# VectorE's instructions as one loop over the heads in a one-query attention kernel

## The chip, the cores and the metric

One core of one Trainium2 chip. The metric is the time of one execution on the device in microseconds (us), the median of several executions. "Span" is the part of it that the profile covers, from the first to the last instruction; it is about 2 us shorter.

## The reference

```python
B, Hq, Hkv, Sq, Sk, D = 1, 32, 8, 1, 65536, 128       # q, k, v in bf16
k = jnp.repeat(k, 4, axis=1); v = jnp.repeat(v, 4, axis=1)
scores = jnp.einsum("bhqd,bhkd->bhqk", q, k) * D ** -0.5
p = softmax(scores, axis=-1)
return jnp.einsum("bhqk,bhkd->bhqd", p, v)
```

One query row per head, 8 groups of 4 query heads, and 65536 keys and values each. K and V together are 268.4 MB, and every byte is used once.

## The kernel before

A head is one of the 8 groups. Its K comes in two tiles of 8.4 MB, and so does its V. VectorE transposes K in place, PE computes scores, VectorE and PE find the maximum, ScalarE takes the exps, VectorE transposes these ("weights"), and PE multiplies them with V. There are three tile buffers in `io`: one for V, two for K. SyncE issues each load when its buffer is free again.

```python
def load_v(g, b):
    done = 2 * (2 * g + b)
    ...                                         # last tiles in pieces
    else:
        SP.wait((s_vc, done))                   # values of the tile before are finished
        load(v, g, b, 0, s_v[0])
        sp.sem_inc(s_v[1], 16)
...
def collect(last=False):                        # "product" and "sum"
    n = DV.mark(dve.tensor_tensor(out=..., in0=vacc, in1=sely..., op=ALU.mult))
    DV.after(n)
    if not last:
        return DV.mark(dve.tensor_reduce(out=vs[:, 0:D], in_=vy[:, :, :], axis=AX.X, op=ALU.add))
...
for g in range(G):                              # unrolled: 8 heads
    for _ in transposes(g, 0): pass
    for i, _ in enumerate(transposes(g, 1)):
        if i == 0 and g:
            DV.wait((s_vc, 4 * g - 2)); weights(g - 1, 1)
    top(g)
    softmax(g)
    if 0 < g < G - 1:
        weights(g, 0)
        DV.wait((s_vc, 4 * g))
        collected[g - 1] = collect()
        ACTQ.wait((s_dv, collected[g - 1]))
        clear(g)                                # ScalarE writes zeros into acc
    elif g: ...
    else:
        weights(g, 0)                           # head 0: nothing to collect
```

PE runs a loop of its own over the tiles. After it comes the end of the last V tile. Its last 24 keys are multiplied one at a time ("singles", a weight load and a 128-column matmul each), and a last fp32 matmul (the "gather") adds what the wide matmuls summed:

```python
for t in range(SL - TAIL, SL):                  # TAIL = 24
    if t in CUTS: pe.wait_ge(s_v[CUTS.index(t)], 16)
    ...
    pe.matmul(out=fin, lhsT=et[:, 1, w0:w0 + H], rhs=io[:, t, :], ...)
pe.wait_ge(s_dv, collected[G - 1])
gather(D, start=False, stop=True).then_inc(s_pe, 1)
```

ScalarE then scales the 4x128 result ("scaling") and stores it.

## Time and profile before

| | before |
|---|---|
| time, median of 3 | 629.8 us (629.76 to 630.69) |
| span of the profiled run | 628.1 us |
| load queue, share of 16 engines | 99.1% |
| first load packet, last load packet | 1.99, 624.47 us |
| last load packet to scaling / scaling to the end of the store / end of the store to the end | 1.10 / 1.22 / 1.35 us |

The page of the kernel before: the span, busy time by engine, the tenths by slice for the DMA engines, and the queue of the loads.

```profile
span 628.1 us, 7091 instructions
PE 346.7 (55%) x2120; PEld 136.0 (22%) x2120; DVE 339.2 (54%) x132; ACT 36.1 (6%) x32; POOL 7.5 (1%) x40
...
DMA  8999999999999999999999999999999999999996
...
q1 hardware_dynamic: 6656, 268.45, 99.1%
```

No compute engine is busy over 55%, and the DMA engines are always busy. The same kernel by stretches (start:end, length, busy us and number of instructions by engine, granted PE clock, DMA share, GB/s):

```profile
core 0: us, PE busy (x) PEld busy (x) DVE busy (x) ACT busy (x) POOL busy (x), PEclk, DMA share, GB/s
2.00:624.00 622.00, 345.25 (x2102) 135.00 (x2102) 337.94 (x129) 35.14 (x31) 6.41 (x33) 0.82 1.00 431
618.00:622.00 4.00, 1.37 (x21) 0.35 (x16) 0.00 (x0) 0.00 (x0) 0.00 (x0) 1.00 0.98 393
622.00:626.00 4.00, 3.08 (x38) 1.68 (x38) 1.48 (x4) 0.36 (x1) 0.00 (x0) 1.00 0.42 142
```

The first row says that 622 of 628 us are loads at a DMA share of 1.00. So only three things can change the time: the rate of the stream, a hole in it, and its two ends.

A middle head (timeline: start, duration, engine, line, operation, and in brackets the idle time before and what ended it):

```profile
363.87 1.97 ACT L247 ACTIVATE ex<-acc,nmb 128x2048 bf16<-128x2048 f32 x1 [68.70 <-DVE nmb L245]
365.96 1.25 DVE L269 STREAM_TRANSPOSE et<-ex 128x1024 bf16<-128x1024 bf16 x1 [2.13 <-ACT ex L247]
367.13 1.01 DVE L275 TENSOR_TENSOR vy<-acc,sely 128x512 f32<-128x512 f32 x1
368.18 0.69 DVE L281 TENSOR_REDUCE vs<-vy 128x128 f32<-128x512 f32 x1
368.90 2.31 ACT L258 ACTIVATE acc<-wz 128x2560 f32<-128x2560 bf16 x1 [2.97 <-DVE vs L281]
371.68 0.59 PE L374 MATMUL pf<-vs,sel 128*4 128x130 f32 x2 [8.04 <-PEq L114]
```

After the exps come weights, product and sum on VectorE, then the clear on ScalarE, then PE's gather.

The end of the chain that ended last (start, duration, what):

```profile
623.56 0.61 PE pf L479 x8
624.17 0.03 issue
624.20 1.05 PE pf L479 x16
625.25 0.23 PE pf L374 x2
...
625.57 0.36 ACT o L341
```

Sixteen singles took 1.05 us, 66 ns each, then the gather.

### The profile page before, as it was taken

Reading aid. Unit: us, or ns where it says so; the run is one execution under the profiler, and the core shown is the slowest. Engines: PE = TensorE matmul, PEld = TensorE weight load, DVE = VectorE, ACT = ScalarE, POOL = GpSimd, SP = SyncE. Lnnn points to the kernel's source line nnn. Section 1 sums busy time; section 2 is a strip of 40 time slices with the busy share of each in tenths; the row PEclk is TensorE's granted clock in tenths of the full one; section 3 lists DMA queues with packets and bytes.
Section 4 is the critical chain, followed back from the end, with each engine's and each line's share of the span. In section 5 each row is a group of like instructions: output and inputs, shape, how many; then the busy total and the mean of one; then the engine's idle time right before and its main releaser. Section 6 shows DMA issues by size and latency. Waiting matters only on the chain. (4 is left out here: it accounts for less than half of the span.)

```text
span 628.1 us, 7091 instructions
## 1 busy us (share of the span) xinstructions
PE 346.7 (55%) x2120; PEld 136.0 (22%) x2120; DVE 339.2 (54%) x132; ACT 36.1 (6%) x32; POOL 7.5 (1%) x40
## 2 busy tenths in 40 slices
PE   0776473725838257382674816648076571876344
PEld 0322131311313023130221302213022230332112
DVE  3984836549065490654807558085570846684210
ACT  0000200020000200002000020000200002000100
POOL 1000000000000000000000000000000000000000
PEclk9999696976969769597695967969679696999658
DMA  8999999999999999999999999999999999999996
GB/s 368 434 467 401 467 401 467 401 447 422 426 442 430 438 430 438 430 438 426 442 413 455 409 459 401 467 401 467 401 463 405 463 405 463 402 435 434 434 434 271
DMA packets 6714, 268.48 MB, mean 427 GB/s; under 512 B 824, under 2 KB 1080, under 8 KB 1464
## 3 DMA queue, kind: packets, MB, share of 16 engines
q1 hardware_dynamic: 6656, 268.45, 99.1%
q8 instruction: 1, 0.02, 0.0%
q10 hardware_dynamic: 56, 0.01, 0.0%
q14 instruction: 1, 0.01, 0.0%
HBM read 268.44 MB, written 0.01 MB: 427 GB/s over the span
## 5 line engine op out<-in xcount | busy, mean ns | idle before, releaser
L422 PE MATMUL acc<-io,wz 128*128 x1024 | 268.5, 413 | 184.3 <-PEq L114 180.6
L228 DVE STREAM_TRANSPOSE io<-io 128x4096 uint32<-128x4096 uint32 (+1 forms) x54 | 279.1, 5207 | 164.7 <-DMA io<-in_k_dram 164.7
L422 PEld LDWEIGHTS acc<-io,wz 128*128 x1024 | 105.1, 103 | 347.8 <-issue 267.9
L380 PE MATMUL acc<-io,et 128*16 128x512 bf16 x1018 | 67.8, 409 | 23.6 <-PEq L114 22.2
L233 DVE TENSOR_REDUCE mg<-acc 128x1 f32<-128x2048 f32 x8 | 18.3, 2292 | 52.8 <-PE acc L422 52.8
L247 ACT ACTIVATE ex<-acc,nmb 128x2048 bf16<-128x2048 f32 x8 | 15.7, 1967 | 531.4 <-DVE nmb L245 531.4
L374 PE MATMUL pf<-vs,sel 128*4 128x130 f32 (+1 forms) x20 | 5.5, 374 | 62.6 <-PEq L114 62.6
L380 PEld LDWEIGHTS acc<-io,et 128*16 128x16 bf16 x1018 | 26.3, 94 | 62.1 <-issue 37.7
L269 DVE STREAM_TRANSPOSE et<-ex 128x1024 bf16<-128x1024 bf16 x16 | 19.6, 1225 | 29.5 <-ACT ex L247 14.9
L258 ACT ACTIVATE acc<-wz 128x2560 f32<-128x2560 bf16 x7 | 16.1, 2307 | 17.9 <-DVE vs L281 17.8
L374 PEld LDWEIGHTS pf<-vs,sel 128*4 128x4 f32 x20 | 1.2, 83 | 63.0 <-issue 63.0
L275 DVE TENSOR_TENSOR vy<-acc,sely 128x512 f32<-128x512 f32 x8 | 7.8, 980 | 12.0 <-PE acc L380 12.0
L237 DVE TENSOR_REDUCE m<-pt 1x4 f32<-1x128 f32 x8 | 2.2, 278 | 21.2 <-PE pt L464 21.2
L360 POOL COPY wz<-qT 32x16 bf16<-32x16 bf16 x32 | 6.1, 191 | 517.8 <-PE acc L422 435.3
L449 PE MATMUL pt<-et 128*16 128x512 bf16 x16 | 6.3, 395 | 0.0
L281 DVE TENSOR_REDUCE vs<-vy 128x128 f32<-128x512 f32 x7 | 4.8, 686 | 0.2
L466 PE MATMUL pb<-ident,nrow 1*128 1x1 f32 x8 | 1.5, 189 | 5.7 <-PEq L114 5.7
L464 PE MATMUL pt<-ident,mg 128*1 128x128 f32 x8 | 2.3, 283 | 2.5 <-PEq L114 2.5
L191 DVE MEMSET acc<- 128x2560 f32 x1 | 2.2, 2192 | 1.6 <-SPq L62 1.6
L245 DVE COPY nmb<-pb 128x1 f32<-128x1 f32 x8 | 1.3, 158 | 3.0 <-PE pb L466 3.0
L466 PEld LDWEIGHTS pb<-ident,nrow 1*128 1x128 f32 x8 | 1.1, 134 | 7.1 <-issue 7.1
L294 ACT ACTIVATE fall<-pf 4x130 f32<-4x130 f32 x7 | 1.9, 269 | 7.5 <-PE pf L374 7.5
(28 smaller groups left out, 16.4 us busy)
## 6 DMA issues: line engine op xcount, KB each, us to landing
io<-in_v_dram SPq DMA_DIRECT2D x5, 4096.0 KB, 16.8
io<-in_k_dram SPq DMA_DIRECT2D x4, 4096.0 KB, 25.9
io<-in_k_dram SPq DMA_DIRECT2D x4, 2048.0 KB, 40.3
io<-in_v_dram SPq DMA_DIRECT2D x1, 2048.0 KB, 10.7
io<-in_v_dram SPq DMA_DIRECT2D x1, 1024.0 KB, 12.9
io<-in_v_dram SPq DMA_DIRECT2D x3, 256.0 KB, 13.3
io<-in_v_dram SPq DMA_DIRECT2D x2, 128.0 KB, 13.2
io<-in_k_dram SPq DMA_DIRECT2D x13, 43.9
```

The source lines that it names most:

```text
L228: dve.transpose(out=part, in_=part).then_inc(s_kt, n // 32)
L233: dve.tensor_reduce(out=mg[:, :], in_=sc, axis=AX.X, op=ALU.max).then_inc(s_mg, 1)
L247: n = ACTQ.mark(act.activation(out=ex[:, :, :].rearrange("p b n -> p (b n)"), in_=sc, func=ACT.Exp, bias=nmb[:, :], scale=SCALE, accum_out ...
L258: cleared[g] = ACTQ.mark(act.activation(out=acc[:, :], in_=wz[:, 0, 0:1].to_broadcast([P, 5 * 512]), func=ACT.Copy))
L269: dve.transpose(out=et[:, :, :].rearrange("p i n -> p (i n)"), in_=ex[:, 2 * b:2 * b + 2, :].rearrange("p i n -> p (i n)"),).then_inc(s_et, 1)
L275: n = DV.mark(dve.tensor_tensor(out=vy[:, :, :].rearrange("p d y -> p y d") if not last else vz, in0=vacc, in1=sely[:, :, None].to_broadca ...
L281: return DV.mark(dve.tensor_reduce(out=vs[:, 0:D], in_=vy[:, :, :], axis=AX.X, op=ALU.add))
L360: gp.tensor_copy(out=wz[r, :, c0:c0 + H].rearrange("p (s w) h -> p s w h", s=2), in_=qTb[r, :, :, g, :],).then_inc(s_w, 1)
L374: return pe.matmul(out=pf[0:H, 0:w], lhsT=sel[:, :], rhs=vs[:, 0:w], skip_group_check=True, **kw)
L380: return pe.matmul(out=vacc[32 * c:32 * c + 16, :, :], lhsT=et[:, ch // 2, w0:w0 + 16], rhs=io[:, PS * ch + 4 * tt:PS * ch + 4 * tt + 4, : ...
L422: i = pe.matmul(out=bass.AP(acc, r_o, [[2560, P], [1, 512]]), lhsT=bass.AP(wz, r_w + ((2 * s + e) * WB - 4 * u), [[4 * WB, P], [1, P]]), r ...
L449: pe.matmul(out=pt[0:16, :], lhsT=et[:, 0, 0:16], rhs=et[:, 0, :], start=True, stop=True)
```

## The change

The intent is a shorter and more regular VectorE program: a loop of 36 instructions for all heads in place of a straight line (155 instructions with its setup and end). The product is taken while ScalarE does the exps. VectorE, not ScalarE, copies each head's result. ScalarE's last clear covers 512 columns only. The last 32 keys are singles, and the gather stands before the last four of them. To make the body the same for every head, all K transposes are 128x4096, most waits count a semaphore down, and head 0 does a dummy sum, product and weights transpose. Cut to its core:

```diff
-TAIL = 24
+TAIL = 32
-        elif ... else:
-            SP.wait((s_vc, done))
-            load(v, g, b, 0, s_v[0])
-            sp.sem_inc(s_v[1], 16)
+            values_done(done)          # SyncE waits, and passes the news to VectorE (s_vd)
+            load(v, g, b, 0, s_v[0])
-    for g in range(G):                 # the unrolled heads shown above
-        ...
+    with nc.body("dve_head", valid_engines=only_d):
+        ...                            # registers
+        y_sum()                        # waits for the last clear, then the sum
+        transposes(0, 0, SL)
+        d_take(s_ga)
+        DV.mark(dve.tensor_copy(out=bass.AP(fall, f, ...), in_=pf[0:H, 0:W]))
+        transposes(1, 0, 128)
+        d_take(s_vd)
+        weights(1)
+        transposes(1, 128, SL)
+        ...                            # maximum, as before
+        d_take(s_vd)
+        dve.tensor_tensor(out=vy..., in0=vacc, in1=sely..., op=ALU.mult).then_inc(s_dv, 1)
+        d_take(s_ex)
+        weights(0)
+        nc.br_cmp(r_g, G, "dve_head", "dve_tail", "IS_LT", engines=only_d)
+        part = acc[:, 2048:2560] if g == G - 1 else sc if g == 0 else acc[:, :]   # the clear
@@ singles
+        if t == CUTS[-2]:
+            pe.wait_ge(s_dv, d_last)
+            gather(D, start=False, stop=False)
```

More of the change, by code (lines that the diff above doesn't have):

```diff
@@ L12 @@
 PE = mybir.EngineType.PE
+DVE = mybir.EngineType.DVE
+POOL = mybir.EngineType.Pool
 P = 128
@@ L109 @@
     s_sc, s_pe, s_vb, s_vc = sem("s_sc"), sem("s_pe"), sem("s_vb"), sem("s_vc")
+    s_sd, s_vd, s_pt, s_ex, s_ds = sem("s_sd"), sem("s_vd"), sem("s_pt"), sem("s_ex"), sem("s_ds")
+    s_cl, s_ga = sem("s_cl"), sem("s_ga")
     def down(eng, which, s, n, wait=False):
@@ L134, in load, with values_done @@
         ).then_inc(s, 16)
-    k_cuts = {(0, 0): [0, 128, 256], (0, 1): [0, 128, 256], (G - 1, 1): [0, 64, 128, 192, 256]}
-    s_k = {(b, lo): sem(f"s_k{b}_{lo}") for b, lo in ((0, 0), (0, 128), (1, 0), (1, 64), (1, 128), (1, 192))}
-    k_count = {}
-    k_ready = {}
+    k_lo = {0: [0, 128], 1: [0, 64, 128, 192]}
+    s_k = {(b, lo): sem(f"s_k{b}_{lo}") for b in k_lo for lo in k_lo[b]}
     def load_k(g, b):
         SP.wait((s_sc, 16 * g - 8 + 8 * b if g else 0))
-        cuts = k_cuts.get((g, b), [0, SL])
+        if g == 1:
+            sp.sem_inc(s_k[b, 128], 16 * (G - 1 - b))
+        cuts = [0, 128, SL] if g == 0 else [0, 64, 128, 192, SL] if (g, b) == (G - 1, 1) else [0, SL]
         for lo, hi in zip(cuts, cuts[1:]):
-            k_ready[g, b, lo] = key = s_k[b, lo], k_count.get((b, lo), 0) + 16
-            k_count[b, lo] = key[1]
-            load(k, g, b, 1 + b, key[0], lo, hi)
+            load(k, g, b, 1 + b, s_k[b, lo], lo, hi)
+    def values_done(n):
+        SP.wait((s_vc, n))
+        if n:
+            sp.sem_inc(s_vd, 1)
     def load_v(g, b):
@@ L153, in load_v @@
             load(v, g, b, 0, s_v[0], CUTS[0], CUTS[1])
-            SP.wait((s_vc, done))
-            for s in s_v[2:4]:
-                down(sp, mybir.EngineType.SP, s, 16)
+            values_done(done)
+            down(sp, mybir.EngineType.SP, s_v[2], 16)
             for lo, hi, s in list(zip(CUTS, CUTS[1:], s_v))[1:]:
@@ L159, in load_v @@
         elif (g, b) in ((G - 2, 1), (G - 1, 0)):
-            for i in range(2):
-                SP.wait((s_vc, done - 1 + i))
-                load(v, g, b, 0, s_v[i], 128 * i, 128 * i + 128)
+            SP.wait((s_vc, done - 1))
+            load(v, g, b, 0, s_v[0], 0, 128)
+            values_done(done)
+            load(v, g, b, 0, s_v[1], 128, SL)
         else:
-            SP.wait((s_vc, done))
+            values_done(done)
             load(v, g, b, 0, s_v[0])
-            sp.sem_inc(s_v[1], 16)
     load_k(0, 0)
     load_k(0, 1)
-    for s in s_v[2:4]:
-        sp.sem_inc(s, 16)
     for g in range(1, G):
@@ L184 @@
     GP.mark(gp.memset(vs[:, :], 0.0))
+    GP.mark(gp.memset(ex[:, :, :], 0.0))
+    GP.mark(gp.memset(vy[:, :, :], 0.0))
     n = GP.mark(gp.memset(ident[:, :], 0.0))
@@ L190 @@
     ))
-    n = DV.mark(dve.memset(acc[:, :], 0.0))
-    collected = {-2: n, -1: n}
+    gp.sem_inc(s_vd, 2)
+    gp.sem_inc(s_cl, 1)
+    for s, n in ((s_k[1, 64], 16 * (G - 1)), (s_k[1, 192], 16 * (G - 1)), (s_v[1], 16 * (2 * G - 3)), (s_v[2], 16)):
+        gp.sem_inc(s, n)
+    DV.mark(dve.memset(acc[:, :], 0.0))
     DV.wait((s_gp, p_ident))
@@ L210, with d_sum, d_nmb, d_out @@
         ))
+    def d_sum(g):
+        return d_qT + 4 * g + 1
+    def d_nmb(g):
+        return d_qT + 4 * g + 3
+    def d_out(g):
+        return d_qT + 4 * g + 4
+    d_last = d_sum(G) + 7
     qTb = qT[:, :, :].rearrange("p s n -> p (s n)").bitcast(bf16).rearrange(
@@ L215 @@
     )
-    def transposes(g, b):
-        for t0 in range(0, SL, 128):
-            if (g, b, t0) in k_ready:
-                DV.wait(k_ready[g, b, t0])
-            n = 128 if 1 < g < G - 1 and b == 0 else 64
-            for t in range(t0, t0 + 128, n):
-                if t > t0 and (g, b, t) in k_ready:
-                    DV.wait(k_ready[g, b, t])
-                part = io[:, (1 + b) * SL + t:(1 + b) * SL + t + n, :]
-                part = part.rearrange("p t d -> p (t d)").bitcast(u32)
-                dve.transpose(out=part, in_=part).then_inc(s_kt, n // 32)
-            yield
@@ L231, in top @@
-    def top(g):
-        DV.wait((s_sc, 16 * g + 16))
-        dve.tensor_reduce(out=mg[:, :], in_=sc, axis=AX.X, op=ALU.max).then_inc(s_mg, 1)
-    def softmax(g):
-        DV.wait((s_pe, 3 * g + 2))
-        n = DV.mark(dve.tensor_reduce(
-            out=m4[:, :], in_=pt[0:1, 0:P].rearrange("o (x h) -> o h x", h=H), axis=AX.X, op=ALU.max
-        ))
-        DV.after(n)
-        dve.tensor_scalar_mul(
-            out=nrow[:, :, :], in0=m4[:, None, :].to_broadcast([1, 32, H]), scalar1=-SCALE
-        ).then_inc(s_nr, 1)
-        DV.wait((s_pe, 3 * g + 3))
-        d_nmb = DV.mark(dve.tensor_copy(out=nmb[:, :], in_=pb[:, 0:1]))
-        ACTQ.wait((s_dv, d_nmb))
-        n = ACTQ.mark(act.activation(
-            out=ex[:, :, :].rearrange("p b n -> p (b n)"), in_=sc, func=ACT.Exp,
-            bias=nmb[:, :], scale=SCALE, accum_out=vs[:, D + g % 2:D + g % 2 + 1],
-        ))
-        exped[g] = n
-        if g == 0:
-            ACTQ.wait((s_gp, p_ident))
-            ACTQ.after(n)
-            clear(0)
@@ L257, in clear @@
-    def clear(g):
-        cleared[g] = ACTQ.mark(act.activation(
-            out=acc[:, :], in_=wz[:, 0, 0:1].to_broadcast([P, 5 * 512]), func=ACT.Copy
-        ))
-    exped = {}
-    cleared = {}
-    def weights(g, b):
-        if b == 0:
-            DV.wait((s_ac, exped[g]))
-        dve.transpose(
-            out=et[:, :, :].rearrange("p i n -> p (i n)"),
-            in_=ex[:, 2 * b:2 * b + 2, :].rearrange("p i n -> p (i n)"),
-        ).then_inc(s_et, 1)
-    def collect(last=False):
-        n = DV.mark(dve.tensor_tensor(
-            out=vy[:, :, :].rearrange("p d y -> p y d") if not last else vz, in0=vacc,
-            in1=sely[:, :, None].to_broadcast([P, 4, D]), op=ALU.mult,
-        ))
-        DV.after(n)
-        if not last:
-            return DV.mark(dve.tensor_reduce(
-                out=vs[:, 0:D], in_=vy[:, :, :], axis=AX.X, op=ALU.add
-            ))
-        n = DV.mark(dve.tensor_tensor(
-            out=vz[:, 0:2, :], in0=vz[:, 0:2, :], in1=vz[:, 2:4, :], op=ALU.add
-        ))
-        DV.after(n)
-        return DV.mark(dve.tensor_tensor(
-            out=vs[:, 0:D], in0=vz[:, 0, :], in1=vz[:, 1, :], op=ALU.add
-        ))
@@ L292, in keep @@
-    def keep(g):
-        ACTQ.wait((s_pe, 3 * g + 7))
-        return ACTQ.mark(act.activation(out=fall[:, g, :], in_=pf[0:H, 0:D + 2], func=ACT.Copy))
-    for g in range(G):
-        for _ in transposes(g, 0):
-            pass
-        for i, _ in enumerate(transposes(g, 1)):
-            if i == 0 and g:
-                DV.wait((s_vc, 4 * g - 2))
-                weights(g - 1, 1)
-        top(g)
-        softmax(g)
-        if 0 < g < G - 1:
-            weights(g, 0)
-            DV.wait((s_vc, 4 * g))
-            collected[g - 1] = collect()
-            ACTQ.wait((s_dv, collected[g - 1]))
-            clear(g)
-        elif g:
-            DV.wait((s_vc, 4 * g))
-            DV.after(collect())
-            collected[g - 1] = DV.mark(dve.memset(vacc, 0.0))
-            weights(g, 0)
-        else:
-            weights(g, 0)
-        if g:
-            n_kept = keep(g - 1)
@@ L321 @@
-    DV.wait((s_ac, n_kept), (s_vc, 4 * G - 2))
-    weights(G - 1, 1)
-    o7 = io[0:H, SL:SL + G - 1, :]
-    for i in range(2):
-        n = DV.mark(dve.reciprocal(out=r7[:, i::2], in_=fall[:, i::2, D + i]))
-    DV.after(n)
-    n = DV.mark(dve.tensor_tensor(
-        out=o7, in0=fall[:, :, 0:D], in1=r7[:, :, None].to_broadcast([H, G - 1, D]),
-        op=ALU.mult,
-    ))
-    SP.wait((s_dv, n))
-    sp.dma_start(
-        out=out[0, 0:(G - 1) * H, 0, :].rearrange("(g h) d -> h g d", h=H), in_=o7
-    ).then_inc(s_st, 16)
@@ L336 @@
-    DV.wait((s_vb, 2 * G))
-    collected[G - 1] = collect(True)
-    DV.wait((s_pe, 3 * G + 2))
-    d_rl = DV.mark(dve.reciprocal(out=rl[:, :], in_=pl))
-    ACTQ.wait((s_dv, d_rl), (s_pe, 3 * G + 3))
-    n = ACTQ.mark(act.activation(out=o[:, :], in_=fin, func=ACT.Copy, scale=rl[:, :]))
-    ACTQ.after(n)
-    act.dma_start(out=out[0, (G - 1) * H:G * H, 0, :], in_=o[:, :]).then_inc(s_st, 16)
-    ACTQ.wait((s_st, 32))
-    for g in range(G):
-        if g == 0:
-            GP.wait((s_dv, d_qT))
-            GP.after(p_ident)
-        else:
-            GP.wait((s_sc, 16 * g))
-        for a in range(4):
-            r = slice(32 * a, 32 * a + 32)
-            c0 = 28 + 32 * a
-            if a == 3:
-                GP.wait(
-                    (s_dv, collected[g - 2]), (s_ac, cleared.get(g - 1, 0))
-                )
-            gp.tensor_copy(
-                out=wz[r, :, c0:c0 + H].rearrange("p (s w) h -> p s w h", s=2),
-                in_=qTb[r, :, :, g, :],
-            ).then_inc(s_w, 1)
@@ L364, with take @@
-    GP.wait((s_sc, 16 * G), (s_dv, collected[G - 2]), (s_ac, exped[G - 1]))
-    gp.sem_inc(s_w, 4)
-    def take(s, n):
-        down(pe, PE, s, n, wait=True)
+    def take(eng, which, s, n=1):
+        down(eng, which, s, n, wait=True)
     IO = 3 * SL * D
@@ L400 @@
     with block("pe_head"):
-        take(s_w, 4)
-        gather(D + 2, start=True, stop=True).then_inc(s_pe, 1)
+        take(pe, PE, s_w, 4)
+        gather(D + 2, start=True, stop=True).then_inc(s_ga, 1)
         nc.br("pe_tile", engines=only)
@@ L417 @@
         r_o = o8 * 16
-        take(s_kt, 1)
+        take(pe, PE, s_kt, 1)
         for u in range(2):
@@ L435 @@
     with block("pe_values"):
-        take(s_et, 1)
+        take(pe, PE, s_et, 1)
         for ch in range(4):
@@ L440 @@
             elif ch != 1:
-                take(s_v[ch // 2], 16)
+                take(pe, PE, s_v[ch // 2], 16)
             for tt in range(16 if ch < 3 else (SL - TAIL) % PS // 4):
-                if (ch, tt) == (3, 8):
-                    pe.wait_ge(s_v[3], 16)
                 i = wide(ch, tt)
@@ L462 @@
     with block("pe_softmax"):
-        take(s_mg, 1)
-        pe.transpose(out=pt[0:1, 0:P], in_=mg[:, :], identity=ident[:, :]).then_inc(s_pe, 1)
-        take(s_nr, 1)
+        take(pe, PE, s_mg, 1)
+        pe.transpose(out=pt[0:1, 0:P], in_=mg[:, :], identity=ident[:, :]).then_inc(s_pt, 1)
+        take(pe, PE, s_nr, 1)
         pe.transpose(
             out=pb[:, 0:1], in_=nrow[:, :, :].rearrange("o x h -> o (x h)"), identity=ident[0:1, 0:1]
-        ).then_inc(s_pe, 1)
+        ).then_inc(s_pt, 1)
         nc.br("pe_head", engines=only)
@@ L472 @@
         out=pl, lhsT=sel[:, :], rhs=vs[:, D + (G - 1) % 2:D + (G - 1) % 2 + 1], start=True, stop=True
-    ).then_inc(s_pe, 1)
+    ).then_inc(s_pt, 1)
     for t in range(SL - TAIL, SL):
@@ L477 @@
             pe.wait_ge(s_v[CUTS.index(t)], 16)
+        if t == CUTS[-2]:
+            pe.wait_ge(s_dv, d_last)
+            gather(D, start=False, stop=False)
         w0 = t % PS // 4 * 32 + 16 + 4 * (t % 4)
-        pe.matmul(
-            out=fin, lhsT=et[:, 1, w0:w0 + H], rhs=io[:, t, :], start=(t == SL - TAIL), stop=False,
-            skip_group_check=True,
-        )
-    pe.wait_ge(s_dv, collected[G - 1])
-    gather(D, start=False, stop=True).then_inc(s_pe, 1)
+        i = pe.matmul(
+            out=fin, lhsT=et[:, 1, w0:w0 + H], rhs=io[:, t, :], start=(t == SL - TAIL),
+            stop=(t == SL - 1), skip_group_check=True,
+        )
@@ new lines, with d_take, transposes, weights @@
+    i.then_inc(s_pe, 1)
+    def d_take(s, n=1):
+        take(dve, DVE, s, n)
+    def transposes(b, lo, hi):
+        for t in range(lo, hi, 64):
+            if t in k_lo[b]:
+                d_take(s_k[b, t], 16)
+            part = io[:, (1 + b) * SL + t:(1 + b) * SL + t + 64, :].rearrange("p t d -> p (t d)").bitcast(u32)
+            dve.transpose(out=part, in_=part).then_inc(s_kt, 2)
+    def weights(b):
+        dve.transpose(
+            out=et[:, :, :].rearrange("p i n -> p (i n)"),
+            in_=ex[:, 2 * b:2 * b + 2, :].rearrange("p i n -> p (i n)"),
+        ).then_inc(s_et, 1)
@@ new lines, in y_sum @@
+    def y_sum():
+        d_take(s_cl)
+        DV.mark(dve.tensor_reduce(out=vs[:, 0:D], in_=vy[:, :, :], axis=AX.X, op=ALU.add))
+    only_d = OrderedEngineSet([DVE])
+    r_g, r_f = (nc.alloc_registers(r, engines=only_d) for r in ("g", "f"))
+    W = D + 2
+    nc.regs_mov(r_g, 0)
+    nc.regs_mov(r_f, (G - 4) * W)
+    nc.br("dve_head", engines=only_d)
+    with nc.body("dve_head", valid_engines=only_d):
+        nc.regs_alu(r_g, r_g, 1, op=ALU.add)
+        nc.regs_alu(r_f, r_f, W, op=ALU.add)
+        nc.regs_alu(r_f, r_f, (G - 1) * W, op=ALU.mod)
+        f = nc.snap(r_f, engines=only_d, donate=True, min_val=0, max_val=(G - 2) * W)
+        y_sum()
+        transposes(0, 0, SL)
+        d_take(s_ga)
+        DV.mark(dve.tensor_copy(
+            out=bass.AP(fall, f, [[(G - 1) * W, H], [1, W]]), in_=pf[0:H, 0:W]
+        ))
+        transposes(1, 0, 128)
+        d_take(s_vd)
+        weights(1)
+        transposes(1, 128, SL)
+        d_take(s_sd)
+        dve.tensor_reduce(out=mg[:, :], in_=sc, axis=AX.X, op=ALU.max).then_inc(s_mg, 1)
+        d_take(s_pt)
+        dve.tensor_reduce(
+            out=m4[:, :], in_=pt[0:1, 0:P].rearrange("o (x h) -> o h x", h=H), axis=AX.X, op=ALU.max
+        ).then_inc(s_ds, 1)
+        d_take(s_ds)
+        dve.tensor_scalar_mul(
+            out=nrow[:, :, :], in0=m4[:, None, :].to_broadcast([1, 32, H]), scalar1=-SCALE
+        ).then_inc(s_nr, 1)
+        d_take(s_pt)
+        dve.tensor_copy(out=nmb[:, :], in_=pb[:, 0:1]).then_inc(s_dv, 1)
+        d_take(s_vd)
+        dve.tensor_tensor(
+            out=vy[:, :, :].rearrange("p d y -> p y d"), in0=vacc,
+            in1=sely[:, :, None].to_broadcast([P, 4, D]), op=ALU.mult,
+        ).then_inc(s_dv, 1)
+        d_take(s_ex)
+        weights(0)
+        nc.br_cmp(r_g, G, "dve_head", "dve_tail", "IS_LT", engines=only_d)
@@ new lines @@
+    nc.switch_bb("dve_tail")
+    DV.n = d_out(G - 1)
+    y_sum()
+    DV.wait((s_ga, 1))
+    DV.mark(dve.tensor_copy(out=fall[:, G - 2, :], in_=pf[0:H, 0:W]))
+    ACTQ.n = G
+    for g in range(G):
+        ACTQ.wait((s_dv, d_nmb(g)))
+        act.activation(
+            out=ex[:, :, :].rearrange("p b n -> p (b n)"), in_=sc, func=ACT.Exp,
+            bias=nmb[:, :], scale=SCALE, accum_out=vs[:, D + g % 2:D + g % 2 + 1],
+        ).then_inc(s_ac, 1)
+        ACTQ.wait((s_ac, g + 1))
+        act.sem_inc(s_ex, 1)
+        if g == 0:
+            ACTQ.wait((s_gp, p_ident))
+        ACTQ.wait((s_dv, d_out(g)))
+        part = acc[:, 2048:2560] if g == G - 1 else sc if g == 0 else acc[:, :]
+        act.activation(
+            out=part, in_=wz[:, 0, 0:1].to_broadcast([P, part.shape[1]]), func=ACT.Copy
+        ).then_inc(s_cl, 1)
@@ new lines @@
+    DV.wait((s_vd, 1))
+    weights(1)
+    o7 = io[0:H, SL:SL + G - 1, :]
+    DV.after(DV.n)
+    for i in range(2):
+        n = DV.mark(dve.reciprocal(out=r7[:, i::2], in_=fall[:, i::2, D + i]))
+    DV.after(n)
+    n = DV.mark(dve.tensor_tensor(
+        out=o7, in0=fall[:, :, 0:D], in1=r7[:, :, None].to_broadcast([H, G - 1, D]),
+        op=ALU.mult,
+    ))
+    SP.wait((s_dv, n))
+    sp.dma_start(
+        out=out[0, 0:(G - 1) * H, 0, :].rearrange("(g h) d -> h g d", h=H), in_=o7
+    ).then_inc(s_st, 16)
@@ new lines @@
+    DV.wait((s_vb, 2 * G))
+    n = DV.mark(dve.tensor_tensor(
+        out=vz, in0=vacc, in1=sely[:, :, None].to_broadcast([P, 4, D]), op=ALU.mult
+    ))
+    DV.after(n)
+    n = DV.mark(dve.tensor_tensor(
+        out=vz[:, 0:2, :], in0=vz[:, 0:2, :], in1=vz[:, 2:4, :], op=ALU.add
+    ))
+    DV.after(n)
+    n = DV.mark(dve.tensor_tensor(
+        out=vs[:, 0:D], in0=vz[:, 0, :], in1=vz[:, 1, :], op=ALU.add
+    ))
+    assert n == d_last
+    DV.wait((s_pt, 1))
+    d_rl = DV.mark(dve.reciprocal(out=rl[:, :], in_=pl))
@@ new lines @@
+    ACTQ.wait((s_dv, d_rl), (s_pe, 1))
+    n = ACTQ.mark(act.activation(out=o[:, :], in_=fin, func=ACT.Copy, scale=rl[:, :]))
+    ACTQ.after(n)
+    act.dma_start(out=out[0, (G - 1) * H:G * H, 0, :], in_=o[:, :]).then_inc(s_st, 16)
+    ACTQ.wait((s_st, 32))
+    for g in range(G):
+        if g == 0:
+            GP.wait((s_dv, d_qT))
+            GP.after(p_ident)
+        else:
+            GP.wait((s_sc, 16 * g))
+            gp.sem_inc(s_sd, 1)
+        for a in range(4):
+            r = slice(32 * a, 32 * a + 32)
+            c0 = 28 + 32 * a
+            if a == 3 and g == 1:
+                take(gp, POOL, s_et)
+            if a == 3:
+                GP.wait((s_dv, d_sum(g)))
+            gp.tensor_copy(
+                out=wz[r, :, c0:c0 + H].rearrange("p (s w) h -> p s w h", s=2),
+                in_=qTb[r, :, :, g, :],
+            ).then_inc(s_w, 1)
@@ L488 @@
+    GP.wait((s_sc, 16 * G))
+    gp.sem_inc(s_sd, 1)
+    GP.wait((s_dv, d_sum(G)))
+    gp.sem_inc(s_w, 4)
 _INS = ['q', 'k', 'v']
```

## The prediction

The forecast came to 629.7 us, 0.1 us under the 629.8 us of the kernel before. The bound rests on the trace alone (431 GB/s at a DMA share of 1.00). The estimated 3.5 us of the last V tile is what the table of DMA issues gives: its last pieces landed 13.2 us after their issue, and the 4.2 MB of its second half take 9.7 us at 433 GB/s.

> **What bounds the kernel now.** The loads of K and V. The queue table gives 268.45 MB on the load queue, 99.1% of 16 engines' time. The table by stretches shows a DMA share of 1.00 and 431 GB/s from 2 to 624 us; load packets overlap without a gap from about 2.0 to 624.5 us of the 628.1 us span. A 64 KB packet took a median of 2.42 us; 16 at a time give 433 GB/s. [...] No compute engine is busy over 55%.
>
> Only two pieces are not streaming: about 2 us before the first packet and 3.6 us after the last (single matmuls, gather 0.23, scaling 0.36, final store about 2.1).
>
> **What the change does.**
> - VectorE becomes a loop. All 64 transposes are now 128x4096 at about 4.4 us,: about 281 us. It gains a dummy sum, product and weights transpose and eight small copies of about 0.2 us that ScalarE did (7 x 0.27): VectorE from 339 to about 344 us, from 132 to about 154 instructions.
> - The product (1.0 us) moves under the exps (1.97 us), and the clear (2.31 us) no longer waits for weights transpose, product and sum (2.97 us of ScalarE idle per middle head). The gather opening the next head should come about 2 us earlier. But PE then needs a transposed K tile, and VectorE is free for that when it was before (exp end + 3 us).
> - The last clear covers 512 columns, replacing a 0.48 us memset. ScalarE falls from 36 to about 34 us. POOL gains two memsets at the start (estimated 2 to 3 us, from 0.63 us for 640 columns), hidden, as the first K half lands at 13.1 us.
> - 32 single slots: the wide part ends one 256 KB piece earlier, so the last sum is ready about 0.3 us sooner, and the gather precedes the last four singles. In the chain of before, the last 16 singles run back to back from 624.20 for 1.05 us, then the gather. Reordering gains 0 to 0.3 us.
>
> **On the critical path.** Nearly nothing. In steady state an 8 MB V tile landed a median 29.2 us after its issue, against about 19.4 us of transfer: some 10 us of backlog. The last V tile has an estimated 3.5 us. [...] The queue should never run dry, and the same bytes at the same rate take the same 622.5 us.
>
> **Prediction.** 629.7 us, range 629.0 to 630.7. Chance of faster by over 2%: 0.005; within 2%: 0.985; slower by over 2%: 0.01.
>
> **What would show it.** Load packets still gapless, DMA share 0.99, about 431 GB/s; span 627.6 to 628.6. VectorE about 344, ScalarE about 34 us. ScalarE's idle before the clear near 0 instead of 2.97 us; gather about 2 us earlier after each exp. Last landing near 624.5; the chain still ends V load, singles, scaling, store.
>
> **What would make it wrong.** A gap in the load queue: a VectorE wait stuck behind a SyncE step, so that a V load goes out after the queue has drained; the last tile would show it first. [...]

## More of the kernel before

The start of head 1, where there is nothing to collect, and the second V load of SyncE (timeline again):

```profile
65.27 1.25 DVE L269 STREAM_TRANSPOSE et<-ex 128x1024 bf16<-128x1024 bf16 x1 [2.12 <-ACT ex L247]
66.44 13.06 DVE L228 STREAM_TRANSPOSE io<-io 128x4096 uint32<-128x4096 uint32 x3
71.46 4.88 PE L422 MATMUL acc<-io,wz 128*128 x14 [2.76 <-PEq L114]
...
95.10 0.33 SPq L132 DMA_DIRECT2D io<-in_v_dram  x1
```

## The result, and the profile after

The changed kernel took 631.1 us (median of 6 runs, 629.75 to 632.25), the kernel before 629.96 us (6 runs). The ratio of fast runs is 1.0014, 95% interval 1.0000 to 1.0029. A ratio here is the mean time of one kernel's fast runs over that of the other's of the same rounds, so it is not quite the ratio of the medians. Executions over 1.5% slower than the fastest of the same kernel are left out of the means. The median lies 0.4 us above the top of the predicted range.

The same lines of the changed kernel. The page:

```profile
span 629.5 us, 7271 instructions
PE 348.6 (55%) x2126; PEld 137.9 (22%) x2126; DVE 345.3 (55%) x154; ACT 34.4 (5%) x26; POOL 9.7 (2%) x42
...
DMA  8999999999999999999999999999999999999995
...
q1 hardware_dynamic: 6656, 268.45, 98.8%
```

By stretches, columns as before:

```profile
core 0: us, PE busy (x) PEld busy (x) DVE busy (x) ACT busy (x) POOL busy (x), PEclk, DMA share, GB/s
2.00:624.00 622.00, 346.08 (x2100) 135.63 (x2101) 343.98 (x151) 33.42 (x25) 8.44 (x36) 0.81 1.00 431
618.00:622.00 4.00, 1.96 (x25) 0.41 (x17) 0.00 (x0) 0.00 (x0) 0.00 (x0) 0.91 1.00 400
622.00:626.00 4.00, 3.70 (x40) 3.10 (x41) 1.47 (x4) 0.00 (x0) 0.00 (x0) 0.57 0.32 108
```

The stream is the same: 431 GB/s at a share of 1.00, with the last packet at 624.47 us in both kernels. The last row differs: the granted PE clock is 0.57 here and was 1.00.

The middle head (timeline):

```profile
364.34 1.06 DVE L419 TENSOR_TENSOR vy<-acc,sely 128x512 f32<-128x512 f32 x1
364.39 1.97 ACT L436 ACTIVATE ex<-acc,nmb 128x2048 bf16<-128x2048 f32 x1 [72.94 <-DVE nmb L416]
366.56 2.31 ACT L446 ACTIVATE acc<-wz 128x2560 f32<-128x2560 bf16 x1
366.64 1.25 DVE L372 STREAM_TRANSPOSE et<-ex 128x1024 bf16<-128x1024 bf16 x1 [1.23 <-DVEq L119]
369.01 0.69 DVE L380 TENSOR_REDUCE vs<-vy 128x128 f32<-128x512 f32 x1 [1.13 <-DVEq L119]
370.10 0.59 PE L248 MATMUL pf<-vs,sel 128*4 128x130 f32 x2 [6.06 <-PEq L119]
```

The product runs under the exps and the clear follows them at once. The gather starts 5.71 us after the start of the exps (370.10 - 364.39) and started 7.81 us after it before (371.68 - 363.87): 2.1 us sooner.

The start of head 1 and the second V load:

```profile
66.07 1.25 DVE L372 STREAM_TRANSPOSE et<-ex 128x1024 bf16<-128x1024 bf16 x1 [1.23 <-DVEq L119]
68.08 0.69 DVE L380 TENSOR_REDUCE vs<-vy 128x128 f32<-128x512 f32 x1 [0.77 <-DVEq L119]
68.68 8.76 DVE L369 STREAM_TRANSPOSE io<-io 128x4096 uint32<-128x4096 uint32 x2
...
73.74 2.72 PE L296 MATMUL acc<-io,wz 128*128 x6 [3.98 <-PEq L119]
...
97.44 0.33 SPq L137 DMA_DIRECT2D io<-in_v_dram  x1
```

Here the change costs something. VectorE waits for the clear and does a sum of zeros before the first transposes, so they start at 68.68 instead of 66.44 us, PE's scores at 73.74 instead of 71.46, and the second V load goes out at 97.44 instead of 95.10.

The end of the chain that ended last:

```profile
623.35 2.68 PE pf L354 x28
626.03 0.22 PE pf L248 x2
626.25 0.24 PE pf L354 x4
...
626.58 0.36 ACT o L483
```

Twenty-eight singles took 2.68 us, 96 ns each on average. While the clock was 0.5, until 625.55 us, they started 107 ns apart in the trace, and the last ones, at 1.0, 56 ns apart. Before, at 1.0, all started 56 ns apart (with the end of the last one, 66 ns each for 16).

The records of barrier instructions are in the trace, although not counted as busy. Those of VectorE in the final barrier (start us, duration ns, instruction):

```
before  627.656   21  EVENT_SEMAPHORE      changed  628.673   21  EVENT_SEMAPHORE
        627.766   10  DRAIN                         629.184  134  DRAIN
        628.092   21  EVENT_SEMAPHORE               629.484   21  EVENT_SEMAPHORE
```

VectorE's drain, the last one of the barrier in the changed kernel, starts 0.11 us after its release in the kernel before, 0.51 us after it in the changed one.

What follows the last load packet, in us:

| | before | changed |
|---|---|---|
| last packet to scaling | 1.10 | 2.11 |
| scaling to the end of the store | 1.22 | 1.22 |
| end of the store to the end of the span | 1.35 | 1.73 |
| sum | 3.67 | 5.06 |

The difference of these two profiled spans (629.5 - 628.1 = 1.4 us) is all here. Two profiles don't make a cause, though: the granted clock can be chance.

### The profile page after: what moved, and what is told of

The parts are those of the page before. It is cut to its first block, busy times and chain, and to the rows that moved or that the text cites. A ratio compares the mean times of both kernels' runs of the same rounds, so it can differ in the third digit from the quotient of the medians.

```text
span 629.5 us, 7271 instructions
## 1 busy us (share of the span) xinstructions
PE 348.6 (55%) x2126; PEld 137.9 (22%) x2126; DVE 345.3 (55%) x154; ACT 34.4 (5%) x26; POOL 9.7 (2%) x42
## 5 line engine op out<-in xcount | busy, mean ns | idle before, releaser
L369 DVE STREAM_TRANSPOSE io<-io 128x4096 uint32<-128x4096 uint32 x64 | 279.6, 4415 | 154.0 <-DVEq L119 154.0
L446 ACT ACTIVATE acc<-wz 128x2560 f32<-128x2560 bf16 (+2 forms) x8 | 16.3, 2040 | 1.0 <-ACT ex L436 0.2
L380 DVE TENSOR_REDUCE vs<-vy 128x128 f32<-128x512 f32 x9 | 6.1, 681 | 7.6 <-DVEq L119 7.6
L419 DVE TENSOR_TENSOR vy<-acc,sely 128x512 f32<-128x512 f32 x8 | 8.5, 1064 | 0.0
L468 DVE TENSOR_TENSOR vy<-acc,sely 128x512 f32<-128x512 f32 x1 | 0.7, 692 | 12.1 <-PE acc L254 12.1
L354 PE MATMUL pf<-io,et 128*4 128x128 bf16 x32 | 3.2, 281 | 0.0
```

The costliest lines, as they stand in the source:

```text
L369: dve.transpose(out=part, in_=part).then_inc(s_kt, 2)
L419: dve.tensor_tensor(out=vy[:, :, :].rearrange("p d y -> p y d"), in0=vacc, in1=sely[:, :, None].to_broadcast([P, 4, D]), op=ALU.mult,).the ...
L446: act.activation(out=part, in_=wz[:, 0, 0:1].to_broadcast([P, part.shape[1]]), func=ACT.Copy).then_inc(s_cl, 1)
```

## The experiments

Eighteen experiments, all correct (some run the same kernel again). The times are the medians of 5 rounds (a few have 4 or 6), and the ratios are to the kernel before. The spread of single runs (a standard deviation of 0.4 us for the kernel before, 0.8 for the changed one) makes one ratio good to about 0.0014, so I also pool the spans. The spans of the kernel before, run beside every call, average 628.19, 628.32, 628.27, 628.26 and 628.36 us in the five calls, so pooling across calls is fair.

### First question: the end with the singles, or the loop?

Theory: the new end (32 singles) costs the time, with chance in PE's clock. Rivals: the VectorE loop costs it; or all is chance. I exchanged the ends of the two kernels and ran both again.

**after_again**: the changed kernel, no edit.

> The changed kernel again, unaltered. Tail theory (32 singles are longer work at the end, and whether PE's granted clock is 0.5 or 1.0 in the last 6 us is a matter of chance): times again spread over 629.7 to 632.3 us with a median near 630.8 to 631.2; if the profile has a granted clock of 1.0 from 622 to 626 us, the chain ends as early as in the kernel before (scaling at about 625.6 us), if 0.5, about 626.5 us. Chance theory (no difference at all): median within 0.2 us of the kernel before. Loop theory [...]: median about 631 whatever the clock in the tail.

Measured: 631.43 us (630.6 to 632.17), ratio 1.0018 (1.0004 to 1.0032). So the slowdown is real, if small. Granted clock from 622 to 626 us: 0.62; last packet to scaling 2.08 us.

**after_tail24**: the changed kernel with the old end.

```diff
-TAIL = 32
+TAIL = 24
-        if t == CUTS[-2]:
-            pe.wait_ge(s_dv, d_last)
-            gather(D, start=False, stop=False)
 ...
+    pe.wait_ge(s_dv, d_last)
+    gather(D, start=False, stop=True).then_inc(s_pe, 1)
```

> The changed kernel with the old end: 24 singles, the last gather after all singles. All of the VectorE loop stays. Tail theory: returns to the kernel before, 629.8 to 630.2 us. Loop theory: stays at about 631 us. Chance theory: like all others.

Measured: 631.4 us (630.52 to 631.99), ratio 1.0015 (1.0001 to 1.0029). My theory of the tail missed: the old end did not bring the time back.

**before_tail32**: the kernel before with the new end (the reverse of that diff).

> The kernel before with the new end alone: 32 singles, the gather before the last four. VectorE unrolled as before. Tail theory: slower and more spread than the kernel before, about 630.6 to 631.3 us. Loop theory: 629.8 to 630.1 us. Chance theory: like all others.

Measured: 630.47 us, ratio 0.9999 (0.9985 to 1.0012). A second miss for the tail theory. The slowdown goes with the loop.

**before_again**: no edit.

> The kernel before against itself: the noise of the comparison, and a second look at the granted clock in its last 6 us. All theories: 629.7 to 630.2 us, ratio 1.000. Tail theory: if the granted clock from 622 to 626 us is 0.5 here, scaling starts about 0.6 us later than at 625.57 us.

Measured: 630.39 us, ratio 1.0006 (0.9992 to 1.002). This is the noise: two sets of the same kernel differ by 0.06%. Clock 0.72 at the end, last packet to scaling 1.25 us.

In all three profiles with the loop so far, 1.73 or 1.74 us pass from the end of the store to the end, and in all three without it 1.35. That pointed to VectorE's drain.

### Second question: a stall at a fixed place, and PE's clock at the end

**after_pad**: four VectorE instructions (eight waits that are already true) in VectorE's idle time before the end.

```diff
+    for _ in range(8):
+        DV.wait((s_gp, p_ident))
     SP.wait((s_dv, n))
     sp.dma_start(out=out[0, 0:(G - 1) * H, ...], in_=o7)
```

> The changed kernel with four more VectorE instructions (semaphore waits that are already true) in the idle time after the product for the first seven heads. In every profile of a kernel with the VectorE loop so far, VectorE's drain in the final barrier starts 0.51 us after its release instead of 0.11 us, and 1.73 us pass from the last store to the end instead of 1.35 us. Position theory (the 0.4 us is a stall between two instructions at a fixed place in VectorE's instruction sequence): with the place moved by four, the stall falls into idle time; 1.35 us from the last store to the end, and about 0.4 us off the time (630.9 us against about 631.3). Loop theory (having run a loop makes the barrier slow, wherever it stands): still 1.73 us.

Measured: 630.51 us (629.25 to 630.84), ratio 0.9998 (0.9984 to 1.0011). The drain starts 0.11 us after its release, and 1.36 us pass from the end of the store to the end. More instructions made it shorter, so having looped is not enough to cause the stall; a place in VectorE's instruction sequence, as expected, would explain it. Only two lengths of the looped program were tried, this one and the changed kernel's, and the padded trace does not show where the stall went: VectorE has no new gap of that length, only idle time in which it could hide. The page's queue table shows another difference, here of the padded kernel and then of the changed one: 0.02 MB instead of 0.01. An 8192-byte packet of the queue marked "instruction" that came after the end (at 629.85 us in the changed kernel) is now inside the span, at 624.49 us. This does not show a cause: in the changed kernel the packet starts after the stall is over, and after_halves below has the same 0.02 MB, from two packets near 615 us, and still stalls.

```profile
q14 instruction: 2, 0.02, 0.0%
```

```profile
q14 instruction: 2, 0.01, 0.0%
```

**after_warm**: spare matmuls (12, 4 and 4) in PE's gaps while the last V tile arrives.

```diff
+    def warm(here, there, n):
+        nc.br_cmp(r_x, 2 * G + 1, there, here, "IS_LT", engines=only)   # last tile only
+        with block(here):
+            for _ in range(n):
+                pe.matmul(out=pt[0:16, :], lhsT=et[:, 0, 0:16], rhs=et[:, 0, :], start=True, stop=True)
+            nc.br(there, engines=only)
```

> The changed kernel with 12, 4 and 4 spare 128x16x512 matmuls in PE's idle gaps while the last V tile arrives, for nothing but to keep PE busy. Clock theory (the end of the kernel is long when the granted PE clock is 0.5 from 622 to 626 us, as in all three profiles of the changed kernel): granted clock 1.0 there, scaling starts about 1.1 us after the last load packet instead of 1.8 to 2.1 us, time about 0.8 us lower and less spread (630.5 us). If the clock is not the cause: clock 1.0 but scaling still 1.8 us or more after the last packet. 1.73 us from the last store to the end in any case.

Measured: 631.07 us, ratio 1.0012 (0.9999 to 1.0026). The clock was 1.00 at the end and scaling came 1.21 us after the last packet, both as expected; the time was not. Its last packet landed only at 625.47 us, about 1 us later than in most profiles: the stream itself had lost time, and the third question takes that up. The edit also has a side effect: in all four kernels with it the second V load goes out 0.5 to 0.7 us later than without it (here at 98.02 us instead of 97.44). By stretches, this kernel:

```profile
97.00:104.00 7.00, 0.91 (x17) 0.20 (x5) 2.28 (x1) 0.00 (x0) 0.00 (x0) 0.91 1.01 403
...
622.00:626.00 4.00, 3.39 (x44) 2.00 (x42) 1.48 (x4) 0.00 (x0) 0.00 (x0) 1.00 0.53 192
```

The first row, near the second V load, shows 403 GB/s; the padded kernel's 449 in the same stretch is the row below. Such a short stretch must be read with care: the figure moves in steps (between 100 and 104 us, two stretches of 2 us of the kernel before read 33 and 524 GB/s). The changed kernel has 440 there and after_halves_warm below, which lost nothing, 421. The idle time of the engines, counted below, is the better measure.

```profile
97.00:104.00 7.00, 0.26 (x5) 0.00 (x0) 3.06 (x1) 0.00 (x0) 0.00 (x0) 0.80 1.05 449
```

**after_pad_warm**: both edits.

> Both of these edits. If both theories hold: last packet to scaling 1.1 us, last store to end 1.35 us, time 629.6 to 630.1 us, at or a little under the kernel before.

Measured: 630.15 us (629.8 to 631.61), ratio 1.0000 (0.9987 to 1.0014); last packet to scaling 1.19 us, end of the store to the end 1.36 us. The pieces came about as expected; the time is just above the expected 629.6 to 630.1.

**before_warm**: the spare matmuls in the kernel before.

> The kernel before with the spare matmuls. Clock theory: granted clock 1.0 from 622 to 626 us, last packet to scaling 1.0 to 1.1 us in place of 1.1 to 1.25 us, 629.6 to 630.0 us with little spread. If the end of the kernel before is never limited by the clock: 630.2 us as before.

Measured: 630.4 us (630.13 to 630.59), ratio 0.9999 (0.9985 to 1.0012). Clock 1.00, last packet to scaling 1.19 us, not the expected 1.0 to 1.1. No gain in the mean, but the standard deviation of its times is 0.17 us, against 0.47 for the kernel before beside it.

The clock at the end, over the 19 profiles whose end lies in that stretch: where the granted clock from 622 to 626 us was 0.72 or more, scaling came 1.10 to 1.33 us after the last packet (11 profiles); where it was 0.64 or less, 1.26 to 2.35 us (8 profiles, 7 of them 1.76 or more). This holds with 24 and with 32 singles, with and without the loop. Of the profiles without spare matmuls, 5 of 9 with the loop and 3 of 6 without it had the low clock, so the profiles do not show that the loop brings it about.

### Third question: is there more than the stall?

Over the runs so far the padded kernels were 0.9 us shorter (628.5 against 629.4 us in span), but the stall is 0.38 us long. **after_pad2** and **after_again2** repeat the pair on one chip:

> The padded version of the changed kernel again. So far the spans of unpadded kernels with the loop average 629.4 us (21 runs), padded 628.5 (10 runs), without the loop 628.25; but the stall that the padding takes away is only 0.38 us long in the traces. If the stall is all, this lies 0.4 us under the unpadded kernel of the same call (630.9 against 631.3 us) and the rest of the earlier difference was chance; if the padding does more, 0.9 us under it.

Measured: 631.11 us, ratio 1.0012 (0.9998 to 1.0025); end of the store to the end 1.36 us.

> The changed kernel, unpadded, for comparison: 631.0 to 631.3 us, 1.73 us from the last store to the end.

Measured: 630.51 us, ratio 1.0002 (0.9988 to 1.0015); end of the store to the end 1.74 us. The order of the two is reversed here. The earlier 0.9 us was then about 0.4 us and luck; pooled, the unpadded kernels with the loop (26 runs of 5 kernels) average 629.22 us in span, the padded ones (15 runs of 3) 628.77, a difference of 0.45 us with a standard error of 0.24.

**before_n64**: the kernel before with all transposes 128x4096, so that its V loads go out at the even distances of the changed kernel.

```diff
-            n = 128 if 1 < g < G - 1 and b == 0 else 64
+            n = 64
```

> The kernel before with all its K transposes 128x4096, as in the changed kernel (the V loads are then issued at even distances of 38.7 us instead of 34 and 43). If the wider spread of the last load packet in kernels with the loop (623.7 to 625.5 us in six profiles, against 624.3 to 624.5 in four without it) comes from when the loads are issued, this kernel spreads like them: standard deviation of its times about 0.7 us instead of 0.4, and mean up to 0.4 us slower than the kernel before. If not: 630.3 us with a deviation of 0.4 or less.

Measured: 630.22 us (629.66 to 631.62), ratio 1.0000 (0.9986 to 1.0013), deviation 0.73. The mean stays; one run of five at 631.62 makes the deviation, so this doesn't decide.

**after_n128**: the padded changed kernel with the first K tile of each head in 128x8192 pieces.

> The padded changed kernel with the first K tile of a head transposed in 128x8192 pieces, as before did for the middle heads (two more padding instructions make up for the two that the loop loses). If issue times make the spread: deviation 0.4 us or less, about 630.2 us. If not: deviation about 0.7 us.

Measured: 638.51 us (638.48 to 638.74), ratio 1.0129 (1.0113 to 1.0144). Neither expectation had this. Two of its stretches:

```profile
102.00:104.00 2.00, 2.00 (x41) 0.96 (x44) 0.89 (x1) 0.00 (x0) 0.00 (x0) 1.00 0.00 0
104.00:106.00 2.00, 1.82 (x33) 0.62 (x25) 2.00 (x1) 0.00 (x0) 0.00 (x0) 1.00 0.00 0
```

The DMA share is 0.00 for 4 us: the queue had run dry, and before that at 41.6 us too. PE can start on a piece only when VectorE has finished it, and a piece is now twice as long (a transpose took 8.69 us instead of 4.42 in the kernel before, which has both); in heads 0 and 1 no backlog hides this. (The kernel before used such pieces only from head 2 on.) Between the bytes that left and the engines that were idle, the trace counts 113 engine-us lost from 4 to 622 us (an engine-us is one of the 16 DMA engines idle for 1 us), 7.1 us of 16 engines.

This made me read the backlog head by head: how long before the earlier loads were through, on the first engine to finish them, was the second V load issued? I call this its margin. Kernels without the loop: 3.8 to 5.0 us. With it (after_n128, at -3.8 us, aside): 1.2 to 2.6 us. With the smallest of these, 1.24 us (after_warm), the trace shows 8.4 engine-us without a load packet between 97 and 104 us; with after_tail24's 1.88 us 2.4, with the changed kernel's 1.94 us 1.2, and with the rest at most 0.1.

**before_late** and **before_late_more** hold VectorE up in head 1 of the kernel before, as the loop does:

```diff
         else:
             weights(g, 0)
+            DV.wait((s_ac, cleared[0]))
+            for _ in range(2):                  # 4 in before_late_more
+                DV.after(DV.mark(dve.memset(vy[:, :, :], 0.0)))
```

> The kernel before, with VectorE held up in head 1 as the loop holds it up: it waits for ScalarE's clear and does two memsets (0.49 us each) before the first K transposes of head 1, which should start near 68.8 us as with the loop, not 66.4. Backlog theory (the second V tile is then issued at 97.4 us with 2.0 us of earlier loads left instead of 4.6, and engines fall apart at that load): margin about 2 us, engines 0.6 to 2 us apart from that load on, mean time 0.3 to 0.6 us over the kernel before and a deviation of 0.6 us or more. If the backlog is of no account: 630.3 us, deviation 0.4.

Measured: 630.69 us (629.94 to 631.84), ratio 1.0006 (0.9992 to 1.002); transposes at 69.19 us, margin 1.84 us, 0.05 engine-us lost; deviation 0.72; mean span 628.70, 0.44 us over the kernel before with a standard error of about 0.35. This does not decide by itself.

> The same with four memsets, 1.1 us later still: margin about 0.9 us. Backlog theory: engines visibly idle around 100 us (10 engine-us or more in all, as in the run with spare matmuls, whose margin was 1.24 us and which lost 8.4), mean 0.7 us or more over the kernel before. If the backlog is of no account: 630.3 us.

Measured: 631.27 us (631.06 to 631.59), ratio 1.0014 (1.0000 to 1.0028); margin 0.24 us (I had said 0.9), 12.9 engine-us lost, mean span 0.94 us over the kernel before. 12.9 engine-us are 0.8 us of 16 engines. So a V load that goes out with too little left in the queue does cost, about what the idle engines say, and a margin of 0.24 us is too little.

**after_halves** gives the changed kernel its backlog back: the second V tile is loaded in two halves, the first as soon as half of the buffer is free.

```diff
-        elif (g, b) in ((G - 2, 1), (G - 1, 0)):
+        elif (g, b) in ((0, 1), (G - 2, 1), (G - 1, 0)):
```

(The counts of `s_v[1]` that POOL gave in advance are given with each load instead.)

> The changed kernel with the second V tile loaded in two halves, the first issued when the first half of the tile before has been used, about 2 us earlier. Backlog theory: margin about 4 us, no idle engines near 100 us, engines at most 0.6 us further apart after that load than before it, mean span about 0.5 us under the unpadded kernels with the loop (629.3 us in 26 runs), so about 628.8; 1.73 us from the last store to the end. If the backlog is of no account: 629.3.

Measured: 631.52 us (629.81 to 631.85), ratio 1.0016 (1.0002 to 1.003). Margin 4.0 us and no idle engines, as wanted, but a mean span of 629.16 us with a deviation of 0.82: a miss.

> The same with the VectorE padding. If backlog and barrier stall are all: span 628.2 to 628.5 us, time 630.0 to 630.3 us, the kernel before or slightly better, deviation 0.4 us.

Measured: 630.35 us (629.72 to 630.73), ratio 0.9996 (0.9983 to 1.001), span 628.44, deviation 0.40, as expected.

**after_halves2** repeats the miss, and **after_halves_warm** adds the spare matmuls.

> after_halves again, because its mean span (629.16 us, deviation 0.82) did not move as the backlog theory wanted, while the margin did (4.0 us). If that was chance: span 628.6 to 628.8 us. If the backlog is not what makes the changed kernel with the loop spread: 629.2 us again, deviation 0.6 or more.

Measured: 630.66 us (630.03 to 632.02), ratio 1.0008 (0.9996 to 1.002); mean span 628.97, deviation 0.81. No chance then: the 11 runs of after_halves average 629.05 us in span, the 16 of the unaltered changed kernel 629.05 as well. A margin of 2.0 us, thin as it looks, costs the changed kernel nothing that I can measure (the standard error of that difference is 0.3 us).

> after_halves with the spare matmuls that keep the PE clock up at the end. If what is left of the spread is the PE clock at the end: span 628.6 to 628.8 us with a deviation of 0.4 or less, last load packet to scaling 1.2 us. If the spread is the load stream's: deviation 0.6 or more although the tail is short. 1.73 us from the last store to the end in both kernels.

Measured: 630.5 us (630.31 to 631.0), ratio 0.9999 (0.9986 to 1.0012); last packet to scaling 1.21 us; mean span 628.78, deviation 0.28. With PE's clock held up at the end and enough backlog, the spread is small, in five runs. Against the kernel before with the same spare matmuls (before_warm, 628.28) the span is 0.50 us longer, with a standard error of 0.15; 0.38 of it is the barrier stall, which this kernel still has (1.74 us from the store to the end). Without the halves the spare matmuls ended at 629.48, with a margin of 1.24 us; with the padding (after_pad_warm, margin 1.85 us) at 628.60.

No version beats the kernel before by more than the noise; after_halves_pad, the best of the loop, is at 0.9996.

## Why the prediction was right or wrong

**The bound, and that nothing in the middle matters: right.** The same bytes took 622.5 us in both profiles (1.99 to 624.47, and 2.00 to 624.47). Both kernels ran at 431 GB/s from 2 to 624 us.

**What the change does inside a head: right, and without effect.** VectorE 345.3 us against 344 predicted, 154 instructions as predicted, ScalarE 34.4 against 34, VectorE's eight copies 0.24 us each against about 0.2, POOL's two memsets 1.81 and 0.52 us, the idle time before the clear gone, the gather 2.1 us sooner.

**The step that failed is "On the critical path. Nearly nothing", in what comes after the last packet.** It took the 3.6 us there as fixed, or up to 0.3 us shorter ("Reordering gains 0 to 0.3 us"). In the profile they became 5.06 us, 1.39 us more than in the kernel before. Two terms were missing from the sum:

1. *The barrier stall, 0.38 us: shown.* In the changed kernel VectorE stalls between two instructions of the final barrier, where nothing is left to hide it. Each of the 8 profiles of unpadded kernels with the loop has 1.73 or 1.74 us from the store to the end, and each of the 12 others 1.35 to 1.37, the 5 padded ones among them. I had thought of a delay at the loop's branch and dismissed it with the slack inside a head, over 6 us before each maximum (6.43 us idle in the timeline of the middle head); I had not asked about the end, where there is none. That it belongs to a fixed place in VectorE's program rests on one change of length. What causes it is not shown: an 8192-byte packet of the instruction queue moved with the padding (624.49 us instead of 629.85), but in the changed kernel that packet starts after the stall.
2. *PE's clock at the end, 1.0 us in the profile: shown that it lengthens the end, not that it differs between the kernels.* At half clock the singles started 107 ns apart instead of 56, and PE, not the data, finished last. I had costed the singles from one profile in which the clock happened to be 1.00. It varied from run to run: from 622 to 626 us it was 0.57 and 0.62 in two profiles of the changed kernel, 1.00 and 0.72 in two of the kernel before. Every recorded interval of granted clock of these two kernels' first profiles (34 and 32 of them) is at 1.0 or 0.5 and, apart from the last one cut off by the end, lasts a whole multiple of 3.41 us. What sets it is shown no further than this: spare matmuls kept it at 1.00 in all four kernels that had them.

**The range was wrong as well.** I took it from three runs of the kernel before (0.9 us from lowest to highest), and their median of 629.8 us was low by luck: 46 later runs average 630.40. So about 0.6 us of the distance from 629.7 us was there before any change. The changed kernel's runs spread over 2.5 us; 8 of its 16 lie inside the predicted range, so where the median of six fell was partly chance. Holding the clock up and giving the backlog back brought the deviation down to 0.28; either alone mostly did not in a kernel with the loop (after_warm 0.53, after_halves 0.86, after_halves2 0.82, but after_halves_pad 0.42). Five or six runs each are few for a deviation.

**The backlog: right in the end, wrong where I looked.** I called the last V tile the tightest (about 3.5 us). The tightest is the second V tile, where the loop leaves about 2.0 of 4.5 us, because head 1 now waits for a clear and a sum of zeros and the load goes out 2.34 us later. It stayed just enough: 2.0 us cost nothing measurable, 1.24 us about 0.7 us (after_warm against after_halves_warm, standard error 0.26), 0.24 us cost 0.9 us, and after_n128, whose queue ran dry twice, lost 8 us.

**The accounts.** Unaltered changed kernel (16 runs) against the kernel before (46 runs beside it): span 629.05 against 628.28, so +0.77 us with a standard error of 0.2; time 630.93 against 630.40, so +0.53 us, because outside the span the kernels with the loop take 1.85 us instead of 2.11. That small saving is measured, its reason isn't. Of the 0.77 us the stall is 0.38. The other 0.4 is within two standard errors of nothing; the slower end at half clock would fill it, but why that should strike the kernel with the loop more often is open. Neither the 32 singles alone (before_tail32, span 628.10) nor the backlog alone (after_halves) could be made to account for it.

## What to carry to other kernels

When a kernel is bound by one stream from beginning to end, look at what comes after the last byte, down to the final barrier, and cost each matmul there at both clocks (here 56 ns from one single to the next at 1.0, 107 ns at 0.5); there a 0.4 us stall counts in full. Rounding off a loop with dummy work in its first turn uses up margin where the queue has not yet built up its backlog (here it left 2.0 us of 4.5 at the second V tile): read the margin of every load, the first ones above all. And take the range of a prediction from how much the changed part can vary, not from how still the old kernel was.
